# Turning the normalised input: paired 32-bit transposes on TensorE, or 16-bit ones for blocks 0 and 1 and VectorE's word transposes through DRAM for blocks 2 and 3

## The chip, the cores and the metric

The kernel runs on one core of a Trainium2 chip. The metric is the device time of one launch in microseconds (us). The engines are TensorE (PE; its weight loads are shown as PEld), VectorE (DVE), ScalarE (ACT), GpSimd (POOL) and SyncE (SP, which issues the DMAs).

## The reference

One layer with two branches in parallel, on x of 2048 rows by 512 columns in bf16:

```python
xn = layernorm(x)                                   # over the 512 columns
qkv = xn @ wqkv                                     # 512 x 1536; 32 heads of 16
# head-wise, each position attends to 8 positions: itself and 2, 4, ... 14 back
logits = einsum("bhsd,bhswd->bhsw", q, k[pos - 2*w]) * 16**-0.5   # masked where pos - 2*w < 0
o = einsum("bhsw,bhswd->bhsd", softmax(logits), v[pos - 2*w])
h = gelu(xn @ w_gate) * (xn @ w_up)                 # 512 x 1376, tanh form
out = x + o @ wo + h @ w_down                       # 512 x 512 and 1376 x 512
```

## The kernel before

The 2048 rows are four blocks (b) of 512, each two pairs (p = 0 to 7) of 256 rows, each two tiles (t = 0 to 15) of 128 rows. For a block the steps are:

- **Input and layer norm.** `ld_x` loads rows into a slot of XIN (four slots of 256 rows; blocks 2 and 3 also use XIN later for the residual input, `ldxr`). For blocks 0 and 1, VectorE takes the statistics (`bnst`, `bnag`), subtracts the mean (`sub`) and scales (`norm`). For blocks 2 and 3, ACT does all of that (lines 746 to 837), and POOL takes the root as a power (`sq`, line 811), whose reciprocal (`rstd`) VectorE forms.
- **Transpose.** `tpx` turns the normalised rows on TensorE (lines 863 to 885) and `evx` copies them to xnT (ACT, line 898). Two neighbouring bf16 columns are read as one 32-bit word, so that two transposes of 128 words turn a tile of 512 columns; the evacuation separates the halves. Feature 4q + k so comes to partition q, and the weights Wqkv, Wg, Wu and Wt are loaded to match: rows 4q to 4q + 3 to partition q. In pair 0 the work is halved (`tpx`, `tpy`; `evx` on ACT, `evy` on VectorE).
- **Projections.** TensorE forms Q, K and V (`mma`, `mmb`, `mmt`, `mmv`, `mm`; lines 941 to 1027), ACT copies them out (`evq`, `evk`, `evv`).
- **Attention.** VectorE multiplies Q with shifted K (`pr`, line 1055, 4.42 us each) and adds (`pa`, `pb`); TensorE adds over heads (`er`); ACT copies the logits out (`lc`). Softmax goes through `d1`, `d2` (VectorE), `exp`, `ln`, `d5` (ACT), `d4`, `d6` (VectorE). The weights go to DRAM (`ss`, pt_scratch) and come back spread over the partitions (`sl`, PT). VectorE multiplies with shifted V (`pv`, line 1207) and adds (`pw`, `pz`; the last of them, line 1227, writes OT).
- **FFN.** `fg` and `fu` on TensorE (line 1245), `gelu` and `uev` on ACT, `h` on VectorE.
- **Output.** TensorE adds `h @ w_down` (`acc...`, line 1337) and `OT @ wo`; in block 3 the latter are tasks of their own at the end (`accw`). ACT copies the sum out (`fe`), VectorE adds x (`fin`), SP stores (`sto`).

Each step is a task on one engine. The program text holds the order of the tasks on each of the five engines, written out (ORDER, line 377). A function (`schedule`, line 169) goes through these orders once, while the program is built, and gives slots of XIN, of the eight PSUM banks and of the other buffers to the tasks in the order in which a model of the durations lets them start; semaphore waits follow from the data and the slots (`assign_sync`). At run time each engine does its list in order.

Of the kernel before, what the change touches and what calls it, by code (L numbers as in the profile page):

```python
# [97 lines left out]
class Graph:  # L98
# [263 lines left out]
    def report(self):  # L362
# [17 lines left out]
        "warm13 warm14 mma0_0 tpx0_1 tpy0_1 mmb0_0 mma0_1 mmt1_0 tpx1_0 mmt1_1 mmt1_2 mmb0_1 tpx1_1 mmt0_2 "  # L380
        "mmt0_3 mmt1_3 mmv0_1 tpx3_0 fg0_0 tpx2_0 fg0_1 fg0_2 fu0_0 fg0_3 mm1_1_0_0 fu0_1 mm1_0_0_0 fu0_2 "
        "fg0_4 mm1_0_2_0 mm1_1_3_0 mm1_0_3_0 mm1_1_2_0 fg0_10 fu0_3 fg1_0 fg0_5 er0_3 mm1_2_3_0 mm1_0_1_0 "
        "mm1_1_1_0 fu0_4 mm1_2_0_0 fu0_5 mm1_2_2_0 fg1_1 fg1_2 fu1_0 fu1_1 fg1_3 mmv0_0 fg1_4 fg1_5 fu1_2 "
        "fu1_3 fg0_6 fg1_6 mmv1_0 fg1_7 fu1_4 fu0_6 mmv1_1 fg0_7 fu0_7 mm1_2_1_0 fg0_8 er1_3 fu0_8 fu1_5 "
        "fg1_8 tpx4_0 fg0_9 fg1_9 fu0_9 fu1_6 tpx5_0 fu1_7 fu1_8 mm2_1_2_0 mm2_0_2_0 mm2_0_0_0 mm2_1_0_0 "
        "mm2_1_3_0 mm2_2_1_0 mm2_0_3_0 mm2_0_1_0 mm2_1_1_0 fu1_9 fg1_10 fg2_0 fg2_1 accd1 fg2_2 accd3 fg2_3 "
        "fu2_0 acca0 fu2_1 fu2_2 accb0 accd2 er2_3 fu2_3 fg2_10 fg2_4 tpx6_0 mm2_2_0_0 tpx7_0 fg2_5 mm2_2_2_0 "
        "fg3_0 mm2_2_3_0 mm3_0_2_0 mm3_0_3_0 mm3_1_2_0 mm3_1_1_0 mm3_0_0_0 fg2_6 mm3_0_1_0 fu2_4 mm3_1_3_0 "
        "fu2_5 fu2_6 fg3_1 mm3_1_0_0 fu3_0 fu3_1 fg3_2 accd7 fg2_7 fu2_7 mm3_2_3_0 acca4 accd6 fg3_3 fg2_8 "
        "mm3_2_0_0 accb4 er3_3 fu3_2 fu3_3 fg3_4 fg3_5 fg2_9 accd5 fu2_8 fu3_4 fg3_6 fu3_5 mm3_2_2_0 fu3_6 "  # L390
        "fg3_7 fu3_7 fu2_9 mm3_2_1_0 fg3_8 fg3_9 fg3_10 fu3_8 fu3_9 acca8 accb8 accd15_0 accd15_2 acca12 "
        "accd11 accd10 accb12 accd9 accd13 accd15_1 accw15_2 accw13 accw15_0 accd14_0 accw12 accw14_0 "
        "accd14_1 accw15_1 accw14_1",
    "act":
        "c_tbl sx1 sq0 negm1 sxx1 evx0_0 sq1 evx0_1 sq2 evq0_0 evx1_0 sq3 evk0_1 evk0_0 evk0_2 evx1_1 evq0_1 "
        "bnst8 sq6 evq0_2 sq4 evq0_3 evk0_3 bnst9 evx3_0 halo1 evx2_0 ve8 gelu0_1 vp8 gelu0_0 bnag8 evk1_0_0 "
        "bnag9 uev0_0 bnst10 uev0_1 sub8 uev0_2 gelu0_4 bnst11 va8 evq1_2_0 gelu0_3 evq1_0_0 ve10 evk1_3_0 "
        "vp10 evk1_2_0 vb8 gelu0_2 uev0_3 uev0_10a gelu0_5 evq1_3_0 gelu0_10 lc0 uev0_10c bnag10 uev0_10b "
        "evk1_1_0 evv1_3_0 exp0 evv0_0_1 uev0_4 bnag11 evq1_1_0 evv1_0_0 ln0 va10 d5_0 uev1_0 uev0_5 uev1_1 "
        "evv1_2_0 gelu1_2 evv0_0_0 gelu1_3 gelu1_0 uev1_2 vb10 gelu1_5 sub9 halo2 sub11 uev1_3 gelu1_4 bnst12 "  # L400
        "gelu1_1 norm9 uev0_6 gelu0_6 evv0_1_1 evv0_1_0 uev1_4 uev0_7 gelu1_6 evv1_1_0 gelu0_7 norm8 gelu1_7 "
        "lc1 sub10 uev1_5 bnst13 evx4_0 norm10 norm11 gelu0_9 uev0_9 uev0_8 evx5_0 gelu0_8 uev1_7 gelu1_8 "
        "uev1_6 ve12 gelu1_9 evk2_2_0 exp1 evk2_3_0 uev1_8 uev1_10b vp12 evk2_0_0 bnag12 evk2_1_0 evq2_0_0 "
        "evq2_1_0 bnag13 evq2_2_0 ln1 bnst14 evq2_3_0 va12 uev1_10a halo3 bnst15 uev1_10c d5_1 ve14 vb12 "
        "sub13 halv1 sub12 vp14 fe1 gelu1_10 gelu2_2 bnag14 sub14 bnag15 gelu2_1 gelu2_0 va14 sub15 vb14 "
        "uev2_0 fe3 fe0 uev1_9 halv2 uev2_2 gelu2_3 uev2_1 norm12 norm13 lc2 uev2_3 norm14 evv2_1_0 norm15 "
        "evx6_0 evx7_0 uev2_10c gelu2_4 evv2_2_0 gelu3_0 uev2_10a fe2 evv2_3_0 gelu2_10 evq3_2_0 gelu2_5 "
        "uev2_10b exp2 evk3_1_0 evv2_0_0 evq3_1_0 evk3_2_0 uev2_4 evk3_3_0 ln2 d5_2 evq3_3_0 evq3_0_0 uev3_1 "
        "uev2_5 uev2_6 evk3_0_0 fe7 uev3_0 gelu3_1 uev2_7 gelu2_7 gelu3_2 gelu2_6 fe6 gelu3_3 fe4 evv3_3_0 "
        "lc3 uev3_3 uev3_10c gelu3_5 uev3_2 gelu3_4 uev3_10b exp3 halv3 uev2_8 ln3 d5_3 evv3_0_0 uev3_4 "  # L410
        "uev3_5 gelu2_9 evv3_2_0 fe5 uev3_7 uev3_6 gelu3_6 gelu3_7 gelu2_8 evv3_1_0 uev2_9 gelu3_9 gelu3_8 "
        "uev3_8 uev3_10a uev3_9 gelu3_10 fe8 fe11 fe10 fe9 fe13 fe12",
    "dve":
        "c_wdz bnst0 bnag0 sub0 rstd0 norm0 mean1 sub1 evy0_0 rstd1 norm1 bnst2 bnag2 sub2 rstd2 evy0_1 norm2 "
        "bnst3 bnag3 sub3 rstd3 norm3 bnst6 bnst4 bnst7 bnag4 bnag6 bnag7 bnst5 sub7 bnag5 rstd6 sub6 norm7 "
        "norm6 sub5 rstd4 sub4 norm5 norm4 pr0_0 pr0_1 pa0 pb0 h0_1 mask d1a_0 d1b_0 d1c_0 d2_0 pr1_1 d4a_0 "
        "h0_10 d4b_0 rstd8 d4c_0 h0_0 d6_0 pr1_0 h0_2 pa1 h1_1 h1_0 pb1 rstd10 pv0_0 d1a_1 h0_3 d1b_1 h1_2 "
        "d1c_1 pv0_1 d2_1 pw0_1 h0_4 pw0_2 d4a_1 pz0 d4b_1 h1_3 d4c_1 pr2_0 d6_1 pr2_1 h1_10 pa2 rstd12 pb2 "
        "pv1_0 rstd14 h2_0 d1a_2 fin0 d1b_2 h1_4 h2_1 d1c_2 pv1_1 d2_2 pw1_1 d4a_2 pw1_2 d4b_2 fin3 d4c_2 pz1 "
        "h2_10 d6_2 pr3_1 pr3_0 fin2 pa3 h2_2 pb3 pv2_1 d1a_3 d1b_3 h2_3 d1c_3 d2_3 pv2_0 d4a_3 h3_0 d4b_3 "  # L420
        "d4c_3 fin4 h3_1 d6_3 pw2_1 h3_2 pw2_2 pz2 fin7 h3_3 h2_4 fin5 h3_4 h3_10 pv3_0 pv3_1 fin8 pw3_1 fin6 "
        "pw3_2 fin11 pz3 fin9 fin1 fin10 fin13 fin15_0 fin15_2 fin12 fin14_0 fin15_1 fin14_1",
    "pool":
        "c_ones c_onef c_id c_vnpad c_eps c_mhalf c_e8a c_e8b c_e8c c_e8d c_ktpad c_mask0 c_mask1 c_utz sq8 "
        "sq10 sq12 sq14",
    "sp":
        "ld_x0_0 ld_x0_1 ld_wq ld_x1_0 ld_wk ld_x3 ld_x1_1 ld_x2 ld_wv ld_x4 ld_wg0 ld_wu0 ld_wu1 ld_x5 "
        "ld_wg1 ld_wt0 ld_wt1 ld_wt2 ldxr0 ld_wd0 ss0_0 ss0_1 ss0_3 ld_x6 ld_x7 ss0_2 sl0_0 ld_wd1 ldxr3 "
        "sl0_1 sl0_2 sl0_3 ld_wo ss1_1 ss1_0 ss1_3 ss1_2 sl1_1 sl1_0 sl1_3 sl1_2 ldxr2 ss2_1 ldxr9 ss2_0 "
        "ss2_3 ldxr4 ss2_2 sto0 sto3 sl2_2 sl2_0 sto2 sl2_3 ldxr7 ldxr10 sl2_1 ldxr5 ldxr12 sto4 ldxr11 ss3_0 "  # L430
        "ss3_3 ss3_2 ss3_1 ldxr13 sl3_0 sl3_1 sl3_3 ldxr14 ldxr6 ldxr8 ldxr1 sl3_2 sto5 sto8 sto7 sto6 sto11 "
        "ldxr15 sto9 sto10 sto1 sto13 sto15_0 sto15_2 sto12 sto14_0 sto15_1 sto14_1",
# [19 lines left out]
def bass_parallel_sum__sliding_local_dilated__glu_gated_geglu__prompt_kernel(nc, A_x, A_wqkv, A_wo, B_x, B_w_gate, B_w_up, B_w_down, out, dbg=None, cfg=None):  # L452
# [31 lines left out]
    TPF = cfg.get("TPF", 1.5)  # L484
# [12 lines left out]
    with contextlib.ExitStack() as es:  # L497
        block = es.enter_context(nc.Block())

        def sb(name, shape, dt):  # L500
            return es.enter_context(nc.sbuf_tensor(name, shape, dt))
# [8 lines left out]
        KT = sb("KT", [128, 2, 4, 528], BF)  # L510
        cf = sb("cf", [128, 128], F32)
# [40 lines left out]
        XINF = XIN.bitcast(F32)  # L552
        PD = nc.dram_tensor("pt_scratch", (4 * 32, 8 * 512), BF, kind="Internal")
# [30 lines left out]
        I_wo = Item("Wo")  # L584
        I_cf = Item("cf")
# [30 lines left out]
            channel_multiplier=1), rd=[I_cf], wr=[I_cf], prio=PC)  # L616
        G.task("pool", "c_mhalf", 0.1, lambda e: e.memset(mhalf[:, :], 0.5), wr=[I_mhalf], prio=PC2)
# [38 lines left out]
        for i, nm in enumerate(("q", "k", "v")):  # L656
            def mk(i=i):
                return lambda e: e.dma_start(
                    Wqkv[:, :, i * 512:(i + 1) * 512],
                    A_wqkv[:, i * 512:(i + 1) * 512].rearrange("(p k) n -> p k n", k=4))  # L660
            t_w = G.task("sp", "ld_w" + nm, 0, mk(), wr=[(I_wq, (nm, 0)), (I_wq, (nm, 1))] if i == 0 else [(I_wq, nm)],
                         prio=(-958, -957.5, -898)[i], nbytes=(900 if i == 0 else 512) * 1024)
            t_ld["w" + nm] = t_w
        I_wt = Item("Wt")
        for (nm, Wx, I_w, src, h) in (("g", Wg, I_wg, B_w_gate, 0), ("u", Wu, I_wu, B_w_up, 0),
                                      ("g", Wg, I_wg, B_w_gate, 1), ("u", Wu, I_wu, B_w_up, 1)):
            def mk(Wx=Wx, src=src, c=slice(640 * h, 640 * h + 640)):
                return lambda e: e.dma_start(Wx[:, :, c], src[:, c].rearrange("(p k) n -> p k n", k=4))
# [4 lines left out]
        for (i, src, c0, c1, o) in ((0, B_w_gate, 1280, 1376, 32), (1, B_w_up, 1280, 1312, 0),  # L673
                                    (2, B_w_up, 1312, 1376, 128)):
            def mk(src=src, c0=c0, c1=c1, o=o):
                return lambda e: e.dma_start(Wt[:, :, o:o + c1 - c0],
                                             src[:, c0:c1].rearrange("(p k) n -> p k n", k=4))
# [22 lines left out]
        for p in range(NP):  # L700
            b = p // 2
            base = LN_BASE[b] + (p % 2) * 10
            it_x = Item("xin%d" % p, P_xin, "x")
            XINI.append(it_x)
# [116 lines left out]
            for t2 in range(2):  # L821
                t = 2 * p + t2
                if p >= PACT:
# [7 lines left out]
                    def mk_nm(t=t, t2=t2, it=it_x):  # L831
# [3 lines left out]
                    G.task("act", "norm%d" % t, 0.6, mk_nm(), rd=[(it_x, t2), (I_rstd, t)], wr=[(it_x, t2)],  # L835
# [15 lines left out]
                def mk_nm(t=t, t2=t2, it=it_x):  # L851
# [3 lines left out]
                t_of["norm%d" % t] = G.task("dve", "norm%d" % t, 0.27, mk_nm(), rd=([I_xs] if t == 1 else xp(it_x, p, t2)) + [(I_rstd, t)],  # L855
# [596 lines left out]
```

## Time and profile before

| | |
|---|---|
| Median of 3 runs | 186.99 us (186.55 to 187.34) |
| The profiled execution | 186.91 us, of which the span of the profile is 185.2 |
| TensorE | 178.7 us busy, 1050 matmuls; clock 1.0 throughout |
| VectorE | 170.3 us busy, 156 instructions |
| ACT | 137.7 us busy, 276 instructions |
| DMA | 20748 packets, 18.03 MB |

Times inside the profile count from the start of the span. A busy TensorE is not yet a TensorE at its peak, because matmuls overlap: what it costs is seen from the start of one group to the start of the next. The same holds, by some 0.08 us an instruction, for VectorE and ACT. Behind an instruction in a timeline stands the idle time of its engine just before it and what ended that, in square brackets.

### The profile page before, as it was taken

What the parts mean: (1) busy time and instruction counts of PE and PEld (TensorE: products, weight loads), DVE (VectorE), ACT (ScalarE), POOL (GpSimd) and SP (SyncE); (2) the same over time, 40 slices, a digit from 0 to 9 for tenths busy, and PEclk for the clock granted to TensorE, in tenths of its full rate; (3) what the DMA queues carried; (4) which work ended last, traced back from release to release, by engine and by line L of the source; (5) the groups of instructions that cost most, each with busy time, mean ns of one, the idle gap of its engine ahead of it and who ended that gap; (6) DMA issues with size and microseconds to landing.
All of it is one profiled execution on the core that took longest, in us unless ns stands there. A gap on an engine that the chain in (4) does not pass through costs nothing.

```text
span 185.2 us, 2759 instructions
## 1 busy us (share of the span) xinstructions
PE 178.7 (97%) x1050; PEld 94.1 (51%) x1068; DVE 170.3 (92%) x156; ACT 137.7 (74%) x276; POOL 20.3 (11%) x22
## 2 busy tenths in 40 slices
PE   8699999999999999999999999999999999999994
PEld 2598444445464555444444554444444444644473
DVE  3789999499998999999989999999999999999943
ACT  5579999899999999999977998537468799112110
POOL 5000003100270000009920000000000000000000
PEclk9999999999999999999999999999999999999999
DMA  3999500360538000002610100146300167501152
GB/s 105 335 349 365 139 2 0 90 226 14 159 100 281 10 0 4 0 2 57 172 58 0 28 0 0 49 124 187 125 0 4 43 147 211 168 0 60 41 168 74
DMA packets 20748, 18.03 MB, mean 97 GB/s; under 512 B 7328, under 2 KB 18560, under 8 KB 20736
## 3 DMA queue, kind: packets, MB, share of 16 engines
q1 hardware_dynamic: 20736, 17.86, 31.6%
q8 instruction: 8, 0.13, 0.3%
q14 instruction: 4, 0.03, 0.1%
HBM read 14.71 MB, written 3.15 MB: 96 GB/s over the span
## 4 chain that ended last, share of the span: by engine, by line
PE 75%; ACT 9%; POOL 6%; DMA 3%; issue 3%; DVE 2%; SPq 1%; DVEq 0%
PE PS L1245 31%; PE PS L1337 21%; PE PS L1024 14%; POOL sq L811 6%; DMA Wqkv<-in_A_wqkv_dram 3%; PE PS L941 3%; PE PS L999 2%; PE PS L869 2%; ACT QT L1035 1%; DVE UNI L1074 1%; PE PS L1284 1%; ACT UT L1300 1%; ACT XS L794 1%; SPq L709 1%; ACT XIN L832 1%
## 5 line engine op out<-in xcount | busy, mean ns | idle before, releaser
L1337 PE MATMUL PS<-Wd,HT 128*128 128x512 bf16 (+2 forms) x204 | 40.1, 345 | 0.2
L1245 PE MATMUL PS<-xnT,Wg 128*128 128x512 bf16 x152 | 38.4, 379 | 0.7 <-ACT VN L1009 0.2
L1245 PE MATMUL PS<-xnT,Wu 128*128 128x512 bf16 x159 | 38.8, 379 | 0.1
L1207 DVE TENSOR_TENSOR UNI<-VN,PT 128x8192 f16<-128x8192 bf16 x8 | 35.3, 4417 | 0.7 <-DMA PT<-pt_scratch 0.7
L1055 DVE TENSOR_TENSOR UNI<-QT,KT 128x8192 f16<-128x8192 bf16 x8 | 35.2, 4415 | 0.0
L1024 PE MATMUL PS<-xnT,Wqkv 128*128 128x512 bf16 x141 | 33.7, 379 | 0.3 <-ACT QT L1035 0.2
L1337 PEld LDWEIGHTS PS<-Wd,HT 128*128 128x128 bf16 x209 | 19.6, 98 | 18.7
L1255 ACT ACTIVATE GG<-PS 128x512 bf16<-128x512 f32 x40 | 23.7, 615 | 4.7 <-DVE HT L1269 3.2
L1370 ACT ACTIVATE OB<-PS 128x512 bf16<-128x512 f32 x14 | 8.4, 598 | 25.3 <-DMA out_dram<-OB 17.2
L1262 ACT ACTIVATE UU<-PS 128x512 bf16<-128x512 f32 x40 | 23.4, 604 | 3.9 <-PE PS L1245 3.8
L811 POOL TENSOR_TENSOR sq<-ve,mhalf 128x2 bf16<-128x2 f32 x4 | 17.8, 4447 | 72.6 <-ACT ve L807 72.6
L1245 PEld LDWEIGHTS PS<-xnT,Wu 128*128 128x128 bf16 x160 | 15.4, 98 | 19.1 <-issue 1.3
L1245 PEld LDWEIGHTS PS<-xnT,Wg 128*128 128x128 bf16 x160 | 15.6, 98 | 17.7 <-ACT VN L1009 0.7
L1024 PEld LDWEIGHTS PS<-xnT,Wqkv 128*128 128x128 bf16 x144 | 16.3, 114 | 15.0 <-ACT GG L1255 0.4
L1067 DVE TENSOR_TENSOR UNI<-UNI 128x8192 f16<-128x8192 f16 x4 | 17.7, 4418 | 0.0
L1216 DVE TENSOR_TENSOR UNI<-UNI 128x8192 f16<-128x8192 f16 x4 | 17.7, 4416 | 0.0
L1337 PE MATMUL PS<-Wo,OT 128*128 128x512 bf16 (+2 forms) x75 | 16.1, 345 | 0.1
L1269 DVE TENSOR_TENSOR HT<-GG,UU 128x1024 bf16<-128x1024 bf16 x20 | 13.4, 682 | 0.0
L898 ACT ACTIVATE xnT<-PS 128x1024 bf16<-128x1024 bf16 (+2 forms) x10 | 8.0, 810 | 3.9 <-PE PS L869 2.3
L1337 PEld LDWEIGHTS PS<-Wo,OT 128*128 128x128 bf16 x76 | 7.0, 98 | 6.8 <-issue 0.4
L1074 DVE TENSOR_TENSOR UNI<-UNI 128x4096 f16<-128x4096 f16 x4 | 9.1, 2282 | 0.0
L1222 DVE TENSOR_TENSOR UNI<-UNI 128x4096 f16<-128x4096 f16 x4 | 9.1, 2280 | 0.0
(97 smaller groups left out, 192.2 us busy)
## 6 DMA issues: line engine op xcount, KB each, us to landing
PT<-pt_scratch SPq DMA_DIRECT2D x16, 256.0 KB, 4.0
out_dram<-OB SPq DMA_DIRECT2D x14, 128.0 KB, 1.8
XIN<-in_A_x_dram SPq DMA_DIRECT2D x12, 128.0 KB, 2.8
Wqkv<-in_A_wqkv_dram SPq DMA_DIRECT2D x3, 512.0 KB, 5.9
XIN<-in_A_x_dram SPq DMA_DIRECT2D x6, 256.0 KB, 5.7
Wg<-in_B_w_gate_dram SPq DMA_DIRECT2D x2, 640.0 KB, 7.5
Wu<-in_B_w_up_dram SPq DMA_DIRECT2D x2, 640.0 KB, 8.8
Wd<-in_B_w_down_dram SPq DMA_DIRECT2D x1, 1280.0 KB, 7.3
```

What stands on the lines that cost most here:

```text
L811: "pool", "sq%d" % t, 5.0, lambda e, t=t, n=n: e.tensor_tensor(out=sq[:, t:t + n], in0=ve[:, t:t + n], in1=mhalf[:, 0:n], op=ALU.pow),
L1024: ins = e.matmul(PS[:, 512 * it.slot:512 * it.slot + 512], lhsT=wcols(which, kt, g), rhs=xnT[:, itx.slot, kt, :], start=(kt == 0), stop=(k ...
L1055: return lambda e: e.tensor_tensor(out=UNI[:, it.slot:it.slot + 2, :, :], in0=bass.AP(QT, (itq.slot * 4 + 2 * h) * 512, [[NQT * 4 * 512, 1 ...
L1067: return lambda e: e.tensor_tensor(out=UNI[:, i0.slot:i0.slot + 2, :, :], in0=UNI[:, i0.slot:i0.slot + 2, :, :], in1=UNI[:, i1.slot:i1.slo ...
L1074: return lambda e: e.tensor_tensor(out=UNI[:, i0.slot, :, :], in0=UNI[:, i0.slot, :, :], in1=UNI[:, i0.slot + 1, :, :], op=ALU.add)
L1207: return lambda e: e.tensor_tensor(out=bass.AP(UNI, ito.slot * 4096, [[NUNI * 4096, 128], [2048, 4], [512, 4], [1, 512]]), in0=bass.AP(VN, ...
L1216: return lambda e: e.tensor_tensor(out=UNI[:, i0.slot:i0.slot + 2, :, :], in0=UNI[:, i0.slot:i0.slot + 2, :, :], in1=UNI[:, i1.slot:i1.slo ...
L1245: ins = e.matmul(PS[0:M, 512 * it.slot:512 * it.slot + 512], lhsT=Wx[:, kt, j * 128:j * 128 + M], rhs=xnT[:, itx.slot, kt, :], start=(kt = ...
L1255: return lambda e: e.activation(out=GG[:, ito.slot, q, :], in_=PS[:, 512 * it.slot:512 * it.slot + 512], func=ACTF.Gelu_apprx_tanh)
L1262: return lambda e: e.activation(out=UU[:, ito.slot, q, :], in_=PS[:, 512 * it.slot:512 * it.slot + 512], func=ACTF.Identity)
L1269: return lambda e: e.tensor_tensor(out=HT[:, ito.slot, j - 1:j + 1, :], in0=GG[:, ig.slot, :, :], in1=UU[:, iu.slot, :, :], op=ALU.mult)
L1337: ins = e.matmul(PS[:, 512 * it.slot:512 * it.slot + CW], lhsT=(OT[:, ito.slot, q, ti * 128:(ti + 1) * 128] if kind == "o" else HT[:, ith. ...
```

## The change

- **Blocks 0 and 1** are transposed in 16 bits: four transposes of 128 columns a tile instead of two of 128 words, with an identity in bf16 (`c_idb`, a cast on POOL). The evacuations read plain columns. `norm0` and `norm1` are split into halves of 256 columns.
- **Blocks 2 and 3** no longer pass TensorE. ACT's `norm` writes its row in a permuted order into a second slot of XIN (`xw`), VectorE transposes 32 x 32 words (`tr4` to `tr7`, one for each pair), SP stores the result to a scratch tensor in DRAM in four parts (`xs`, runs of 64 bf16) and loads it again (`xl`), and ACT's `evx` separates the halves of the words on the way to xnT, from SBUF instead of PSUM.
- **The weights** Wqkv, Wg, Wu and Wt are loaded with rows q, 128 + q, 256 + q and 384 + q on partition q.
- **The orders** of all five engines are written anew. Of them the prediction uses these parts:

```diff
 "pe" after:  ... mm1_1_3_0 fg0_5 fu0_5 er0_3 ... fu3_8 fg3_9 fu3_9 acca8 accb8 acca12 accd10 accd15_2 accb12
              accd15_0 accd14_0 accd11 accd9 accd13 accw15_2 accw15_0 accw13 accw14_0 accw12 accd14_1
              accw14_1 accd15_1 accw15_1
 "act" after: ... uev1_6 evx5_0 evv1_0_0 gelu1_7 ... sub15 norm15 halo3 fe1 fe3 uev1_10c uev1_10b uev1_10a
              fe0 gelu1_10 gelu1_8 gelu2_1 gelu2_2 uev2_0 uev2_1 evv2_0_0 evv2_1_0 gelu1_9 uev2_2 lc2
              uev2_10c evx6_0 fe2 evx7_0 ...
 "dve" after: ... norm0a norm0b ... bnst3 bnag3 evy0_1 sub3 ... pr0_0 pr0_1 pa0 pb0 h0_0 rstd8 mask h0_1 d1a_0
              d1b_0 tr4 d1c_0 d2_0 pr1_0 d4a_0 d4b_0 d4c_0 h0_2 rstd10 d6_0 pr1_1 pa1 tr5 pb1 h0_3 h1_0 h1_1
              pv0_0 ... h1_2 d4c_1 h1_3 tr6 d6_1 rstd14 pr2_0 tr7 pa2 h1_10 pb2 pv1_1 ... fin3 ... fin0 ...
              fin6 ... fin2 ... fin5 ... fin4 pz2 ... fin7 pv3_0 fin1 fin8 pw3_1 fin11 pw3_2 fin10 pz3 fin9 ...
 "sp" after:  ... ld_wg0 ld_wu0 ld_x5 ld_wg1 ld_wu1 ld_wt0 ld_wt1 ld_wt2 xs4_2 xs4_0 ld_x6 xs4_3 xs4_1 ld_wd0
              ss0_1 ... xl4 sl0_0 sl0_2 sl0_1 xs5_0 xs5_1 xs5_2 xs5_3 sl0_3 ld_x7 ldxr0 xl5 xs6_0 ss1_0 ss1_1
              ss1_2 xs6_1 xs6_2 ss1_3 xs6_3 xs7_1 sl1_3 sl1_2 xl6 xs7_2 xs7_3 xs7_0 sl1_0 sl1_1 xl7 ...
```

The core of the code:

```diff
+        ident = sb("ident", [128, 128], BF)
+        XD = nc.dram_tensor("xt_scratch", (8 * 256, 512), BF, kind="Internal")
+        G.task("pool", "c_idb", 0.65, lambda e: e.tensor_copy(out=ident[:, :], in_=cf[:, :]),
 ...
-                    A_wqkv[:, i * 512:(i + 1) * 512].rearrange("(p k) n -> p k n", k=4))
+                    A_wqkv[:, i * 512:(i + 1) * 512].rearrange("(k p) n -> p k n", p=128))
 ...  (the same for Wg, Wu and Wt)
+            it_xw = Item("xw%d" % p, P_xin, "x") if b in TR_DVE else None      # TR_DVE = (2, 3)
 ...  (norm of blocks 2 and 3, on ACT)
+                            return lambda e: e.activation(
+                                out=XIN[:, itw.slot, t2, :].rearrange("q (c i e) -> q e i c", i=32, e=2),
+                                in_=XIN[:, it.slot, t2, :].rearrange("q (e i c) -> q e i c", e=2, i=32),
+                                func=ACTF.Identity, scale=rstd[:, t:t + 1])
 ...
+            if it_xw is not None:
+                G.task("dve", "tr%d" % p, d_dve(512, 1.04), lambda e, it=it_x, itw=it_xw: e.transpose(
+                    out=XINF[:, it.slot, :, :].rearrange("q t (c i) -> q (t c i)", c=8),
+                    in_=XINF[:, itw.slot, :, :].rearrange("q t (c i) -> q c t i", c=8)),
+                for a in range(4):
+                    G.task("sp", "xs%d_%d" % (p, a), 0.64, lambda e, it=it_x, a=a, p=p: e.dma_start(
+                        bass.AP(XD, p * 131072 + 64 * a, [[4096, 32], [256, 16], [1, 64]]),
+                        XIN[32 * a:32 * a + 32, it.slot, :, :].rearrange("q t (c f) -> q (t c) f", f=64)),
+                t_xl = G.task("sp", "xl%d" % p, 0.5, lambda e, itw=it_xw, p=p: e.dma_start(
+                    XIN[:, itw.slot, :, :], bass.AP(XD, p * 131072, [[512, 128], [65536, 2], [1, 512]])),
+                G.task("act", "evx%d_0" % p, 1.05, lambda e, itw=it_xw, itx=XTI[b], o=o: e.activation(
+                    out=xnT[:, itx.slot, :, o:o + 256].rearrange("q (e s) c -> q s c e", e=2),
+                    in_=XIN[:, itw.slot, :, :].rearrange("q s (c e) -> q s c e", e=2), func=ACTF.Identity),
+                continue
 ...  (blocks 0 and 1)
-                            for s in range(2):
-                                c0 = 512 * it.slot + s * 128 * n + q * 128
-                                ins = e.transpose(PS[:, c0:c0 + 128], XINF[:, ito.slot, t2, s:s + 255:2],
-                                                  cf[:, :])
+                            for kt in range(4):
+                                c0 = 1024 * (it, it2)[kt // 2].slot + kt * 128 * n + q * 128
+                                ins = e.transpose(PSB[:, c0:c0 + 128], XIN[:, ito.slot, t2, kt * 128:(kt + 1) * 128],
+                                                  ident[:, :])
```

## The prediction

> **What bounds the kernel now.** First the page, for what is full and where:
>
> ```profile
> PE 178.7 (97%) x1050; PEld 94.1 (51%) x1068; DVE 170.3 (92%) x156; ACT 137.7 (74%) x276; POOL 20.3 (11%) x22
> ...
> DVE  3789999499998999999989999999999999999943
> ACT  5579999899999999999977998537468799112110
> PEclk9999999999999999999999999999999999999999
> ```
>
> Matmuls overlap (379 ns is one's duration, but four 512-column ones start every 0.86 us), so 97% alone proves little. DVE is full from slice 4 to slice 38, and ACT to slice 20. Three engines run close together, so the next view is the gaps: the idle time in VectorE's timeline between its first big product (line 1055, start 16.79) and the last sum of the attention (line 1227, end 176.03).
>
> ```profile
> 34.01 0.29 DVE L1121 TENSOR_TENSOR PS<-PS,mask 32x128 f32<-32x128 f32 x1 [1.09 <-PE PS L1098]
> 35.47 0.43 DVE L1132 TENSOR_TENSOR SU<-PB 128x512 bf16<-128x512 bf16 x1 [1.17 <-ACT PB L1127]
> 43.78 0.69 DVE L1176 TENSOR_TENSOR PB<-EX,rc 128x1024 bf16<-128x1024 f16 x1 [0.44 <-ACT rc L1172]
> 57.95 4.42 DVE L1207 TENSOR_TENSOR UNI<-VN,PT 128x8192 f16<-128x8192 bf16 x1 [0.73 <-DMA PT<-pt_scratch]
> 93.33 0.17 DVE L782 RECIPROCAL rstd<-sq 128x2 f32<-128x2 bf16 x1 [0.58 <-POOL sq L811]
> ...
> 174.81 1.21 DVE L1227 TENSOR_TENSOR OT<-UNI 128x2048 bf16<-128x2048 f16 x1
> ```
>
> In 159 us VectorE waits 4.0 us (1.09 + 1.17 + 0.44 + 0.73 + 0.58); the last 118 us hold one wait. Then TensorE's timeline around that end:
>
> ```profile
> 171.18 5.53 PE L1337 MATMUL PS<-Wd,HT 128*128 128x512 bf16 x32
> 176.54 1.69 PE L1337 MATMUL PS<-Wo,OT 128*128 128x128 bf16 x12
> ```
>
> The product with Wo of block 3 needs that sum and starts at 176.54, with no gap on TensorE before it. VectorE was done 0.5 us earlier; a hand-over takes about 0.2, so 0.3 us is spare. TensorE sets the end, VectorE is 0.3 us behind it as a second bound: time taken off TensorE brings nothing unless VectorE follows.
>
> **The change part by part.** *Blocks 2 and 3 leave TensorE.* The chain of waits holds
>
> ```profile
> 62.25 0.47 PE PS L869 x4
> ```
>
> Four 32-bit transposes turn 256 rows in 0.47 us. Four such pairs go: TensorE -1.88 us. *Blocks 0 and 1 in 16 bits*: eight transposes for four. Sixteen 128-column 16-bit matmuls (line 941) take about 0.90 us in steady state, 0.056 each, so eight cost 0.45 for 0.47: nothing. The Trainium skill ("TensorE: Matmul & The Clock Gate", Part 4: PE-mode transpose) speaks against doubling their number: it gives some 275 ns for a 16-bit transpose inside a kernel. The trace agrees on a single one (283 ns median at line 869), but four end in 0.47 us because they overlap. At 275 ns unoverlapped, the sixteen of block 1 would add some 3.5 us; I leave that out.
>
> *VectorE gets four word transposes* (tr4 to tr7) of 512 32-bit words. The trace has none. Low end: a two-input 16-bit operation on 512 columns, 0.42 us. High end: twice the one-word-per-step price, 1.2. Taken: 0.69, like line 729 (512 columns, 684 ns); line 1381's rows give the same (284 ns at 128, 419 at 256: 1.05 ns per column over 150). Neighbours overlap by 0.08, so 0.61 each, +2.44 us. All four stand ahead of the last attention sum. In VectorE's new order eleven final adds (fin) stand ahead of it where nine did: 2 x 0.34 = +0.68. The split norms of rows 0 to 255 cost 0.17 more each (348 ns whole, 150 for one column at line 742, so about 250 a half), but run before the 1.41 us wait for the input's fourth tile: free; uncovered, 0.34. The copy evy0_1 (0.40, 0.33 of it unoverlapped) moves behind that wait: +0.33 before the first big product. Sum: +3.45.
>
> *What the new order absorbs.* tr4 stands behind the waits for mask and logits, tr5 and tr7 behind a 4.3 us operation, tr6 behind two products of the FFN: none fills an old gap. But h0_1 now stands in the 1.17 wait (0.6), and with a transpose more ahead of pv0_0 the 0.73 wait shrinks by 0.6. Absorbed: 1.2; at most all 4.0, at least 0. Last sum: 176.03 + 3.45 - 1.2 = 178.3.
>
> *The tail on TensorE.* Of the work after that sum (6.05 us now, 176.54 to 182.59), accd14_0 (eleven 256-column matmuls, 1.2 us) moves ahead and accd15_1 (eleven of 128, 0.62) behind: 5.5 us left. TensorE would be ready for it at 176.54 - 1.88 + 1.2 - 0.62 = 175.2, three us before VectorE: so VectorE decides. End of TensorE: 178.3 + 0.2 + 5.5 = 184.0, against 182.6: +1.4 us. What follows (last add, store) is the same.
>
> *The trip through DRAM.* Each pair adds four stores of 64 KB and a 256 KB load. Nearest rows: the pt_scratch stores (64 KB in runs of 256 bytes, 2.2 us to landing, 0.6 to issue), PT loads 4.0, x loads 5.7. One trip: 0.7 + 4 x 0.6 + 2.2 + 0.5 + 4.0 = 9.8 us at 4.0, 11.5 at 5.7, where now the evacuation follows the transposes at once. It is off the path if the statistics run ten us earlier; ACT's new order puts some twenty instructions of about 0.5 between norm15 and evx7_0, so I take 0. On SP's queue the twenty issues (12 us) are in line with others: the stores of pair 7 stand ahead of block 1's PT loads (sl1_3, sl1_2) and wait for tr7. Behind tr7, VectorE has pa2, h1_10 and pb2 (4.34 + 0.33 + 2.2 = 6.9 us) before pv1_1 needs them, and 1.8 of issues plus 4.0 of landing make 5.8: covered by 1.1 us. Stores of pair 4 stand before Wd's load, used 40 us later. Runs of 128 bytes may land slower than 256; +2 us would break that cover. On ACT, a late load stops evx4_0 to evx7_0; behind evx5_0 stand evv1_0 and gelu1_7, whose PSUM banks TensorE then waits for. *ACT*: line 898's copies (1.02 us) read SBUF instead of PSUM; line 1150 (1024 columns from SBUF, 1.06) says +0.04. The norms write in steps of 128 bytes, which no row shows: 0 to a doubling of the 0.42 us that 512 columns take (line 898: 1.02 at 1024, 0.60 at 512): 8 x 0.42 = 3.4 us on an engine full to slice 20; taken 0, like line 832's 0.73. The skill ("SBUF — State Buffer", Door 1) says each access that crosses to another 16-byte line pays a penalty; no run here shows it, and by it ACT would go towards the 3.4.
>
> *Weights in tiles of 128 rows*: runs keep their length and only their order in DRAM changes. Wd is already loaded like that (1280 KB in 7.3 us), Wqkv in rows of four (4.6 to 6.9 for 512 KB under load): taken 0. TensorE waits 1.3 us on Wqkv at the start, so bounds are -0.6 and +1.0. The 16-bit identity costs POOL one cast (0.21 us for 32 columns at line 626, 0.1 of it fixed, so some 0.55 for 128), done by about 2.1; the first transposes start at 4.93: hidden by 2.8 us, and a longer cast would delay them by what it has over that.
>
> **The rivals.** *A, TensorE sets the end and is relieved (faster).* Decides from the point where the new order absorbs nearly all 4.0 us of VectorE's waits. With 2.6 absorbed the end does not move; with 3.5 it is 0.9 us earlier, with all 4.0 it is 1.4: 185.5 us. TensorE's own floor lies below that (175.2 + 5.5 = 180.7, -1.9). For: the orders are written anew on every engine. Against: two of the five waits (rc, POOL's power) stand where no new work goes. *B, it cancels*: 1.7 to 3.5 absorbed, 186.0 to 187.8, about 187. *C, the trip or the strided norms show*: if landings are 2 us late, pv1_1 waits about 1 and the first matmuls of block 3 about 1 more, on top of the forecast: 190.3. For: today block 3 has no lead (norm15 ends at 101.95, its transposes start at 102.00). Against: the margins above.
>
> **How the numbers follow.** The sum stands against the profiled execution, 186.91 us (span 185.2, 1.71 around it), 0.08 under the median 186.99. Forecast: 186.91 + 1.4 = 188.3. Its own range, 0.6 to 1.7 absorbed: 187.8 to 188.9 on the waits alone; transposes at the far 1.2 would add 4 x 0.5 = 2.0 and reach 190.3. About 0.5% (0.93 us) is what a measurement of this kernel can tell from no change. Chances: forecast 0.51, A 0.18, B 0.18, C 0.13. So faster 0.18, same 0.18, slower 0.64. Leaving out half of A and the far half of C, the range is 185.7 to 190.3.
>
> **What would show it.** Right: PE's busy sum about 2 us lower in a longer span; four transposes on DVE near 0.7 us; line of pz3 ending near 178; TensorE now idle in front of the last Wo products or at waits for VectorE. The DMA packets grow by at least 8192 runs of 128 bytes. Wrong: pz3 ending before 177 with DVE's waits gone (A or B); a wait of DVE on PT, or of ACT and PE on xt_scratch's loads, over 1 us, or norms over 1 us (C); TensorE's first Wqkv matmuls more than 0.5 us later, which would be the weights.

## The result, and the profile after

The changed kernel takes 217.65 us (median of 4, 214.88 to 221.44) where the one before, run beside it, takes 186.92. Two of the four executions lie more than 1.5% above the fastest and count as slow, so all comparisons here use the other two, 215.7 us on average: ratio 1.154, interval 1.145 to 1.163, 28.8 us slower. The forecast was 188.3 in a range up to 190.3. The direction was right and the size was wrong by 27 us. The profiled execution of the changed kernel took 218.77 us (span 217.1), 3 us more than that average.

The head of its page, for comparison with the head of the page before:

```profile
PE 187.5 (86%) x1068; PEld 91.8 (42%) x1068; DVE 174.0 (80%) x162; ACT 166.9 (77%) x276; POOL 15.8 (7%) x23
...
PE   8899987899494769999279934999999999999995
...
DVE  4799992899584848963789796179999989999973
ACT  6599999999999989699996898879635776740121
PEclk9999999999999958999859995799999999999999
```

VectorE worked 3.7 us more than before (174.0 against 170.3), ACT 29.2 us more (166.9 against 137.7), in the same number of instructions (276). TensorE and VectorE, full before, now have holes, between slices 7 and 26; in the same slices ACT is at 8 or 9 nearly throughout. The costliest groups show where ACT's time is (busy us, then mean ns of one):

```profile
L841 ACT ACTIVATE XIN<-XIN,rstd 128x512 bf16<-128x512 bf16 x8 | 20.5, 2624 | 0.1
L901 ACT ACTIVATE xnT<-XIN 128x1024 bf16<-128x1024 bf16 x4 | 19.1, 4775 | 0.0
```

The same work in the kernel before (min/median/max in ns):

```profile
L832 ACT ACTIVATE XIN<-XIN,rstd x8: 708/732/778, 53.5 to 101.2; 128x512 bf16<-128x512 bf16 x8
L898 ACT ACTIVATE xnT<-PS x10: 384/1018/1025, 5.4 to 102.8; 128x1024 bf16<-128x1024 bf16 x6, 128x256 bf16<-128x256 bf16 x2, 128x512 bf16<-128x512 bf16 x2
```

Line 841 is the norm of blocks 2 and 3, which writes its row in the permuted order: 2624 ns, where line 832 before took a median of 732. Line 901 is evx, which separates the halves of the words: 4775 ns, where a copy of 1024 columns at line 898 took 1018. So eight norms cost 8 x (2.62 - 0.73) = 15.1 us more and four evx 4 x (4.78 - 1.02) = 15.0: 30.1 us, the whole of ACT's increase (29.2) and about the size of the loss (28.8).

That this work is on the path is seen in the chain that ended last, by engine and line, with ACT at 39% of the span where it had 9%:

```profile
PE 51%; ACT 39%; DVE 4%; issue 3%; DMA 1%; SPq 0%; ACTq 0%; DVEq 0%
```

and in some of its steps in order of time (start, us, engine, line):

```profile
72.54 4.65 ACT xnT L901
...
96.55 4.78 ACT XIN L841 x2
...
128.43 4.65 ACT xnT L901
```

VectorE's largest waits (total us, times, longest) name ACT as releaser: the norm itself, and what stands behind the two lines in ACT's list:

```profile
DVE HT L1321 <- ACT UU L1314: 8.1, 2, 4.9
DVE XIN L888 <- ACT XIN L841: 7.8, 3, 3.7
```

TensorE's longest wait, 6.40 us for evx, is the start of block 3's projections, in its timeline:

```profile
133.12 6.85 PE L1076 MATMUL PS<-xnT,Wqkv 128*128 128x512 bf16 x20 [6.40 <-ACT xnT L901]
```

Neither engine waits for the scratch tensor's loads or for PT anywhere.

### The profile page after: what moved, and what is told of

Same layout as the page of the kernel before. It is cut to its first block, busy times and chain, and to the rows that moved or that the text cites. A ratio compares the mean times of both kernels' runs of the same rounds, so it can differ in the third digit from the quotient of the medians.

```text
span 217.1 us, 2812 instructions
## 1 busy us (share of the span) xinstructions
PE 187.5 (86%) x1068; PEld 91.8 (42%) x1068; DVE 174.0 (80%) x162; ACT 166.9 (77%) x276; POOL 15.8 (7%) x23
## 4 chain that ended last, share of the span: by engine, by line
PE 51%; ACT 39%; DVE 4%; issue 3%; DMA 1%; SPq 0%; ACTq 0%; DVEq 0%
PE PS L1389 21%; PE PS L1297 16%; PE PS L1076 12%; ACT XIN L841 9%; ACT xnT L901 7%; ACT GG L1307 4%; ACT UU L1314 3%; DVE UNI L1107 2%; ACT XIN L833 2%; ACT XS L802 2%; ACT XS L756 1%; ACT PB L1179 1%; ACT xnT L951 1%; ACT L1307 1%; DMA XIN<-in_A_x_dram 1%
## 5 line engine op out<-in xcount | busy, mean ns | idle before, releaser
L1076 PE MATMUL PS<-xnT,Wqkv 128*128 128x512 bf16 x144 | 39.1, 423 | 12.0 <-ACT xnT L901 6.4
L1297 PE MATMUL PS<-xnT,Wg 128*128 128x512 bf16 x160 | 39.1, 379 | 6.1 <-ACT UU L1314 3.4
L1389 PE MATMUL PS<-Wd,HT 128*128 128x512 bf16 (+2 forms) x209 | 41.7, 353 | 0.0
L1314 ACT ACTIVATE UU<-PS 128x512 bf16<-128x512 f32 x40 | 24.4, 630 | 5.4 <-PE PS L1297 3.2
L1297 PEld LDWEIGHTS PS<-xnT,Wu 128*128 128x128 bf16 x160 | 15.1, 98 | 20.2 <-ACT GG L1307 0.9
L841 ACT ACTIVATE XIN<-XIN,rstd 128x512 bf16<-128x512 bf16 x8 | 20.5, 2624 | 0.1
L1389 PE MATMUL PS<-Wo,OT 128*128 128x512 bf16 (+2 forms) x76 | 17.1, 359 | 2.6 <-ACT OB L1422 2.6
L901 ACT ACTIVATE xnT<-XIN 128x1024 bf16<-128x1024 bf16 x4 | 19.1, 4775 | 0.0
L819 POOL TENSOR_TENSOR sq<-ve,mhalf 128x2 bf16<-128x2 f32 x4 | 13.0, 3242 | 77.4 <-ACT ve L815 56.1
L1087 ACT ACTIVATE KT<-PS 128x512 bf16<-128x512 f32 x12 | 7.1, 590 | 5.1 <-PE PS L1076 5.1
```

The lines of the kernel that those rows point to most:

```text
L841: return lambda e: e.activation(out=XIN[:, itw.slot, t2, :].rearrange("q (c i e) -> q e i c", i=32, e=2), in_=XIN[:, it.slot, t2, :].rearr ...
L901: G.task("act", "evx%d_0" % p, 1.05, lambda e, itw=it_xw, itx=XTI[b], o=o: e.activation(out=xnT[:, itx.slot, :, o:o + 256].rearrange("q (e ...
L1076: ins = e.matmul(PS[:, 512 * it.slot:512 * it.slot + 512], lhsT=wcols(which, kt, g), rhs=xnT[:, itx.slot, kt, :], start=(kt == 0), stop=(k ...
L1297: ins = e.matmul(PS[0:M, 512 * it.slot:512 * it.slot + 512], lhsT=Wx[:, kt, j * 128:j * 128 + M], rhs=xnT[:, itx.slot, kt, :], start=(kt = ...
L1314: return lambda e: e.activation(out=UU[:, ito.slot, q, :], in_=PS[:, 512 * it.slot:512 * it.slot + 512], func=ACTF.Identity)
L1389: ins = e.matmul(PS[:, 512 * it.slot:512 * it.slot + CW], lhsT=(OT[:, ito.slot, q, ti * 128:(ti + 1) * 128] if kind == "o" else HT[:, ith. ...
```

## The experiments

The theory after this result: ACT pays for the order in which it writes, and nearly all of the loss is that. The rivals: the price comes from contention with VectorE's transposes or the DMAs; or the rest of the change (new orders, more VectorE work, the trip) carries a good part of the loss.

### The price of an order, alone on the chip (e1)

One kernel without the layer: it runs ACT and VectorE instructions of these shapes, each pattern twice, with nothing beside them.

```diff
+ e.activation(out=B[:, 0:64*511+1:64], in_=A[:, 0:512], func=ACTF.Identity, scale=rs[:, 0:1])   # L51; other lines: other steps
+ e.activation(out=B.."q (c i e) -> q e i c", in_=A.."q (e i c) -> q e i c", ...)                # L57, the norm as changed
+ e.activation(out=.."q (e s) c -> q s c e", in_=A.."q (s c e) -> q s c e", ...)                 # L60, evx as changed
```

> Leaves the whole computation out: ScalarE and VectorE each copy 512 columns (128 partitions, 16 bits, SBUF to SBUF) with a write step or a read step of 1 to 64 elements, and then in the two orders of the changed norm and evacuation, alone on the chip and one after the other. Theory (the write order costs ScalarE, nothing else): dense 0.73 us; written 8 columns at 128 bytes apart as in the changed norm 2.6 us; the 1024-column evacuation with its two halves written alternately 4.8 us, and 1.05 us with the same data written in runs and read at 4 bytes' step. Steps in reading cost nothing. Rival (contention: other engines and DMAs slow the writes in the full kernel): alone, the scattered forms take under 1.2 us. What step the price begins at is open: 16 bytes by the rule on lines of 16 bytes, 4 or 8 bytes otherwise.

Groups by line (busy us of the two, then mean ns of one); lines 45 to 51 write with a step of 1, 2, 4, 8, 16, 32 and 64 elements of two bytes:

```profile
L45 ACT ACTIVATE B<-A,rs 128x512 bf16<-128x512 bf16 x2 | 1.4, 722 | 67.2 <-DVE rs L28 67.2
L46 ACT ACTIVATE B<-A,rs 128x512 bf16<-128x512 bf16 x2 | 1.7, 864 | 0.1
L47 ACT ACTIVATE B<-A,rs 128x512 bf16<-128x512 bf16 x2 | 2.9, 1427 | 0.1
L48 ACT ACTIVATE B<-A,rs 128x512 bf16<-128x512 bf16 x2 | 5.1, 2556 | 0.1
L51 ACT ACTIVATE B<-A,rs 128x512 bf16<-128x512 bf16 x2 | 5.1, 2570 | 0.1
...
L54 ACT ACTIVATE B<-A,rs 128x512 bf16<-128x512 bf16 x2 | 2.4, 1194 | 0.1
L57 ACT ACTIVATE B<-A,rs 128x512 bf16<-128x512 bf16 x2 | 5.1, 2567 | 0.1
L60 ACT ACTIVATE B<-A 128x1024 bf16<-128x1024 bf16 x2 | 9.4, 4710 | 0.1
L61 ACT ACTIVATE B<-A 128x1024 bf16<-128x1024 bf16 x2 | 2.1, 1056 | 0.1
```

The price nearly doubles with the step from 4 to 8 and from 8 to 16 bytes (864, 1427, 2556 ns) and then stays flat up to 128 bytes (2570). That fits a price for each move of the writes to another 16-byte line: at 16 bytes and more, each element is on another line than the one before it, and (2556 - 722) over the 448 moves more than the 64 of a dense row is 4.1 ns a move on top; over all 512 it is 5.0 ns each, fixed cost included. At shorter steps a move costs less (3.7 ns at 8 bytes, 2.2 at 4). The number of lines touched is not what counts: the changed norm touches the 64 lines of a dense row and no others, but moves with every element, and alone takes 2567 (2624 in the kernel). The changed evx takes 4710 (4775); with its two inner loops exchanged, so that it writes runs, evx takes 1056 (L61). Its 1024 moves instead of 128 come to the same 4.1 ns each. Nothing runs beside them here, so contention falls as a cause. Reading pays less: 1194 ns at steps of 16 bytes (L54), 746 at 8 bytes. I had expected steps in reading to cost nothing; that holds up to 8 bytes only.

### The write orders alone, in the kernel before (e2)

```diff
 (norm8 to norm15)
-    out=XIN[:, it.slot, t2, :], in_=XIN[:, it.slot, t2, :],
+    out=XIN[:, it.slot, t2, :].rearrange("q (c i e) -> q e i c", i=32, e=2), in_= (the same),
 (evx of blocks 2 and 3)
-    out=xnT[...].rearrange("q (s e) c -> q s e c", e=2), in_=PSB[...].rearrange("q (s c e) -> q s e c", ...)
+    out=xnT[...].rearrange("q (s e) c -> q s c e", e=2), in_=PSB[...].rearrange("q (s c e) -> q s c e", ...)
```

Each element is read and written where it was; only the order in which ACT steps through them is the change's. (The norm, which works in place, here also reads in steps of 128 bytes, where the change reads a dense row; in e1 such reads alone take 1152 ns, well below the writes.)

> The kernel before, with only the order in which ScalarE writes changed, values the same: norm8 to norm15 in place with steps of 128 bytes, and the evacuations of pairs 4 to 7 with the halves written alternately. No DRAM trip, no transpose on VectorE, old orders. Theory: eight norms at 2.6 instead of 0.73 and four evacuations at 4.8 instead of 1.02, +30 us of ScalarE; 205 to 217 us. Rival (the DRAM trip, SP's queue or the new orders cost the 30 us): 187 to 190 us.

Measured: 215.01 us (214.71 to 215.18) against 187.18, ratio 1.150 (1.147 to 1.152). The two lines from its trace (min/median/max in ns):

```profile
L832 ACT ACTIVATE XIN<-XIN,rstd x8: 2621/2722/2931, 53.8 to 119.1; 128x512 bf16<-128x512 bf16 x8
...
L899 ACT ACTIVATE xnT<-PS x10: 384/1024/5091, 5.4 to 125.8; 128x1024 bf16<-128x1024 bf16 x6, 128x256 bf16<-128x256 bf16 x2, 128x512 bf16<-128x512 bf16 x2
```

ACT's sum goes to 166.3 us (before 137.7), and 28.6 us more on ACT make 27.8 more in the time. Without transposes on VectorE, without the trip and without new orders, nearly the whole loss (28.8) is there.

### The changed kernel with evx writing runs (e3)

```diff
-    out=xnT[...].rearrange("q (e s) c -> q s c e", e=2), in_=XIN[...].rearrange("q s (c e) -> q s c e", e=2)
+    out=xnT[...].rearrange("q (e s) c -> q s e c", e=2), in_=XIN[...].rearrange("q s (c e) -> q s e c", e=2)
```

> The changed kernel with the four evacuations evx4 to evx7 writing each half as a run and reading at a step of 4 bytes; values the same. Theory: each 4.8 becomes about 1.05, ScalarE -15 us, time 201 to 204. Rival (the price is the load of the scratch tensor that they wait for): unchanged at 215 to 218.

Measured: 202.61 us (201.41 to 203.79), ratio 1.083 (1.077 to 1.090) to before. One exchange of two loops, with the same values in the same places, gives back 13.1 us of the 15.0 that the four instructions cost. They take a median of 1052 ns now; the norms still take 2597, and VectorE's transposes still wait 10.0 us in all in front of them, as in the changed kernel (7.8 behind the norms and 2.2 behind a short copy that follows the last of them):

```profile
DVE XIN L888 <- ACT XIN L841: 10.0, 4, 3.7
```

### The norm stepping in shorter strides as well (e5)

```diff
 (e3's edit, and in the norm)
-    out=XIN[...].rearrange("q (c i e) -> q e i c", ...), in_=XIN[...].rearrange("q (e i c) -> q e i c", ...)
+    out=XIN[...].rearrange("q (c i e) -> q e c i", ...), in_=XIN[...].rearrange("q (e i c) -> q e c i", ...)
```

The innermost loop now writes in steps of 4 bytes and reads in steps of 16.

> The changed kernel, values the same, with evx4 to evx7 written in runs and norm8 to norm15 in the order that writes at 4 bytes' step and reads at 16 (1.20 us in the run of patterns, against 2.56 as changed and 0.72 dense). Theory (the price is the number of 16-byte lines written): norms 1.2, ScalarE 3.8 us over the kernel before, time 187 to 191. Rival (the permutation itself or the DRAM trip costs the rest): norms stay near 2.6 or the time stays over 195.

Measured: 188.84 us (188.58 to 189.0), ratio 1.011 (1.007 to 1.015).

```profile
L841 ACT ACTIVATE XIN<-XIN,rstd x8: 1206/1253/1274, 32.3 to 88.7; 128x512 bf16<-128x512 bf16 x8
```

The same permutation at 1253 ns instead of 2604: of the 28.8 us, 26.9 are gone, with no part of the change given up.

### The norm in natural order (e6)

```diff
 (e3's edit, and in the norm)
-    out=XIN[...].rearrange("q (c i e) -> q e i c", ...), in_=XIN[...].rearrange("q (e i c) -> q e i c", ...)
+    out=XIN[:, itw.slot, t2, :], in_=XIN[:, it.slot, t2, :]
```

> The changed kernel with norm8 to norm15 not permuted (dense writes) and evx4 to evx7 in runs; blocks 2 and 3 then pair features with the wrong weights, and only the time is read. What is left is what my sum priced: TensorE -1.88, four word transposes on VectorE, the DRAM trips, the weights and the new orders. My sum said 188.3 and had 0 for the weights, which measured -1.2: 187.1, between 185.5 and 189. Rival (the DRAM trip or SP's queue hurts by itself): over 189.

Measured: 185.29 us (184.98 to 185.89), ratio 0.992 (0.990 to 0.995): 1.6 us *faster* than before (186.86 beside it), just below the range that was expected. The head of its page:

```profile
PE 177.6 (97%) x1050; PEld 92.0 (50%) x1068; DVE 172.7 (94%) x162; ACT 138.1 (75%) x276; POOL 14.8 (8%) x23
```

and VectorE's timeline, its two waits left before the last attention sum, and that sum:

```profile
32.88 0.29 DVE L1172 TENSOR_TENSOR PS<-PS,mask 32x128 f32<-32x128 f32 x1 [0.53 <-PE PS L1149]
34.26 0.42 DVE L1183 TENSOR_TENSOR SU<-PB 128x512 bf16<-128x512 bf16 x1 [0.50 <-ACT PB L1178]
...
174.19 1.21 DVE L1278 TENSOR_TENSOR OT<-UNI 128x2048 bf16<-128x2048 f16 x1
```

With ACT's sum back at 138.1 the loss is gone. VectorE does 2.4 us more than before and ends the sum 0.6 earlier, at 175.40: of its 4.0 us of waits 1.0 are left. The weights alone bring 1.2 us (e4, below), so some 0.4 of the 1.6 is left for the transposes on VectorE, the trip and the new orders together, which is within the intervals. The gain is not one that the change's kernel could collect as written, because its pairing of words needs the permutation; what a norm in natural order would need elsewhere (rows of the weights in another order, another layout of the scratch tensor) was not built.

### The weights alone (e4)

```diff
-    A_wqkv[...].rearrange("(p k) n -> p k n", k=4)
+    A_wqkv[...].rearrange("(k p) n -> p k n", p=128)      (the same for Wg, Wu and Wt; all else as before)
```

> The kernel before with only the weights Wqkv, Wg, Wu and Wt loaded with rows q, 128 + q, 256 + q, 384 + q on partition q; the transposes stay as they were, so features and weights are paired wrongly and only the time is read. My prediction's term: 0, between -0.6 and +1.0 us. In the changed kernel TensorE's first matmuls on Wqkv began earlier than before, so the theory says -0.5 to 0: 186.4 to 187.0. Rival (rows 384 KB apart load slower): +1 us or more.

Measured: 186.0 us (185.47 to 186.42), ratio 0.993 (0.991 to 0.996): 1.2 us faster than 187.18, more than expected. The profiled executions are 0.7 apart (186.24 and 186.91). TensorE's timeline has the first product with Wqkv 0.57 us earlier, with no wait; it started at 6.47 after 0.74 of waiting:

```profile
5.90 0.64 PE L955 MATMUL PS<-xnT,Wqkv 128*128 128x128 bf16 x8
```

Behind a second wait on Wqkv 0.24 of that lead is left (8.73 for 8.97), and at the end it is 0.67: the last product with Wo starts at 181.10 instead of 181.77. In between VectorE waits 3.5 us instead of 4.0: its waits of 0.73 on PT and of 0.58 behind POOL are gone, and two of 0.28 and 0.52 behind ACT are new. The loads of Wg and Wu land 0.6 and 0.8 us sooner (6.9 and 8.0 us against 7.5 and 8.8), but so does that of Wd, which the edit leaves alone (6.7 against 7.3); of the three loads of Wqkv the quickest takes 3.9 us for 4.6 and the median 6.0 for 5.9. Which of these makes the 1.2 us was not settled.

### Sixteen-bit transposes for all four blocks, and these weights (e7)

The kernel before, in its own orders, with the change's code for blocks 0 and 1 used for blocks 2 and 3 as well, and its weights; no transposes on VectorE, no trip.

```diff
-    TR_DVE = cfg.get("TR_DVE", (2, 3))
+    TR_DVE = cfg.get("TR_DVE", ())           (in the changed kernel; ORDER of the kernel before, with norm0a, norm0b, norm1a, norm1b, c_idb)
```

> The first and third part of the change alone, in the old orders: all four blocks turned by TensorE in 16 bits (eight transposes a pair for four), weights with rows q, 128 + q, 256 + q, 384 + q; no word transposes, no DRAM trip. Values right. Theory: transposes equal (0.45 for 0.47 us a pair), weights -1.2: 185.8 to 186.4. Rival (16-bit transposes do not overlap, 275 ns each): +10 us or more on TensorE, over 190.

Measured: 185.45 us (184.93 to 186.14), ratio 0.993 (0.990 to 0.995): faster than both kernels, and below the expected 185.8 to 186.4. In TensorE's timeline eight transposes take what four 32-bit ones took (0.64 at line 869 before):

```profile
15.14 0.61 PE L917 MATMUL PS<-ident,XIN 128*128 128x128 bf16 x8
```

The time is that of e4 within the intervals, so the doubled number of transposes costs nothing that can be measured; the gain is the weights'.

### More work on VectorE, nothing else (e8)

```diff
+ for q in range(9): G.task("dve", "trx%d" % q, ..., e.transpose(out=TRO[:, :], in_=WgF[:, 0, 0:192]))   (the kernel before; nine of them, at four places without idle time)
```

> The kernel before with nine word transposes of 192 columns added on VectorE in its full stretches (two or three at a time, before pw0_1, pw1_1, pr3_1, pw2_1), nobody waits for their result: VectorE +2.5 to 3 us, nothing else changed. Step tested: VectorE is a second bound 0.3 us behind TensorE. Theory: +2 to +2.5 us, 189 to 189.7. Rival (VectorE has slack somewhere behind them): under 188.

Measured: 188.58 us (188.09 to 189.99), ratio 1.011 (1.007 to 1.015): +1.7 us for 2.8 us more of VectorE's busy sum (173.1 against 170.3), under the expected 189 to 189.7 and above the rival's 188. In the profiled execution (189.17 us, above the median) VectorE's last attention sum ends at 178.72 instead of 176.03; 0.45 of these 2.7 us is a later start of the first big product (17.24 for 16.79). TensorE's Wo products that need it start at 178.78 instead of 176.54. On the way TensorE waits for VectorE twice, 0.34 us each, which it did not in the kernel before; the first of these lines is the wait for block 2's sum:

```profile
PE PS L1343 <- DVE OT L1233: 0.3, 1, 0.3
PE PS L1097 <- DVE UNI L1080: 0.3, 1, 0.3
```

So VectorE is a second bound close behind TensorE: work put where it has no idle time shows for the most part. Block 2's sum ends at 158.57 and the waiting product starts at 158.62, so a hand-over for which TensorE stands idle takes 0.05 us, not 0.2, and the 0.5 us by which VectorE was ahead in the profile before leave some 0.45 of spare, not 0.3.

## Why the prediction was wrong

ACT's work and the time, in one table (the two durations are medians of their lines, ACT busy is from each profile, the time is the median, for the changed kernel the average named with the result):

| kernel | norm, evx (ns) | ACT busy (us) | time (us) |
|---|---|---|---|
| before | 732, 1018 | 137.7 | 186.9 |
| changed, norm in natural order (e6) | 722, 1058 | 138.1 | 185.3 |
| changed, short steps (e5) | 1253, 1052 | 142.0 | 188.8 |
| changed, evx in runs (e3) | 2597, 1052 | 152.3 | 202.6 |
| before, with the write orders (e2) | 2722, up to 5091 | 166.3 | 215.0 |
| changed | 2604, 4777 | 166.9 | 215.7 |

- **The step that failed: the ACT term.** It was two terms. The norms' writes in steps of 128 bytes were bounded at "0 to a doubling of the 0.42 us", 3.4 us for eight, and taken as 0; they measured +1.9 us each, 15.1. The doubling had no reason behind it. The order of evx's writes was not seen at all: the text priced only the change of source from PSUM to SBUF (+0.04 us) and missed that the new inner loop jumps between two halves of xnT with every element; it measured +3.76 us each, 15.0. So a term of 0 to 3.6 was 30.1.
- **The cover.** Taking 0 also needed ACT to have room. It had none: in the 90 us from 20 to 110 of the profile before,

```profile
20.00:110.00 90.00, 89.08 (x482) 44.76 (x490) 85.82 (x60) 85.56 (x177) 17.75 (x4) 1.00 0.21 64
```

  ACT, the fourth engine in this line, is busy 85.56 us, as full as VectorE (85.82). The prediction said that ACT is full to slice 20, and then looked for the path on TensorE and VectorE alone. ACT's work there came out in the time at near its price: 28.6 us of work made 27.8 of time in e2, 14.6 less made 13.1 less from the changed kernel to e3, and 10.3 less made 13.8 less from e3 to e5. That the last is more than its price shows that not all of it is ACT's own time: TensorE's granted clock goes from 0.958 to 1.0 in the same step (see the last section). A sum of ACT's extra work that meets the loss so closely is in part luck.
- **The rule that was set aside.** The Trainium skill ("SBUF — State Buffer", Door 1) was quoted with its penalty for each access that crosses to another 16-byte line, and set aside, because no run showed it. It was right in kind: in e1 the price grows up to a step of 16 bytes and is flat from there on. The page's rule gave no size, and ours came from an arbitrary cap. Where the page says that two hits to a line are needed for full bandwidth, two are not enough for ACT's writes: at two to a line (step of 8 bytes) they take 1427 ns for 722, at four 864. ACT's reads agree (746 at two to a line).
- **Rival C and the signs.** "Norms over 1 us" stood among the signs of rival C, and is what the trace shows, but C's 190.3 was built of landings, and no case carried the norms' cost into its time. The landings came as priced: stores of the scratch tensor 2.2 us, its loads 3.5 (taken 4.0; in e6 2.6 and 4.2), and nobody waits for them. The packets grew by 9536, where at least 8192 was named.
- **VectorE's sum.** The transposes were right: 711 ns each against 0.69. The absorption was wrong: 1.2 us taken, and in e6, where ACT doesn't interfere, 3.0 of the 4.0 us of waits are gone (mask 1.09 to 0.53, PB 1.17 to 0.50, rc, PT and POOL's to nothing), two of these at places that the text had called out of reach. With the first big product 0.65 us earlier, the last sum comes 0.6 earlier instead of 2.3 later, and TensorE goes on to the products that need it at 175.59 without a gap. So the waits were absorbed as rival A has it, and 185.3 is about A's time (185.5); behind the ACT term it could not show. But A's gain is not shown to be TensorE's relief: e7, with all transposes on TensorE and the old orders, takes 185.45, the same within the intervals. Against e7, taking blocks 2 and 3 off TensorE cancels, as rival B says, and the gain over the kernel before is the weights', 1.2 of the 1.6 us by e4.
- **Weights.** Taken 0 within -0.6 to +1.0; e4 measured -1.2, outside the bound. The bound was drawn from the wait at the start, of which 0.57 us went; what more there is goes with fewer waits of VectorE further on (3.5 us for 4.0). That the earlier start removed those was not shown: in e8, with the weights as before, the wait on PT is gone as well.
- **The hand-over.** The 0.2 us for it was 0.15 too much by e8's row (0.05), which moves the forecast's end by no more than that.
- **16-bit transposes.** "Nothing" was right. The Trainium skill ("TensorE: Matmul & The Clock Gate", Part 4: PE-mode transpose) gives some 275 ns for one; here one lasts 219 ns (line 917, median in e7), and eight that overlap take 0.61 us together. The 283 ns that the prediction set beside it is that of a 32-bit one.

## What to carry to other kernels

Before pricing an instruction whose access pattern changes, count how often its innermost loop moves the writes to another 16-byte line, for ACT and VectorE alike: with every element on another line than the one before, ACT's norm of 512 columns took 2.6 us for 0.72, and its copy of 1024 took 4.7 for 1.06. Where a permutation must be made, put the long step on the reading side and the short one (4 bytes or less) or the run on the writing side; e3 and e5 got 26.9 of 28.8 us back by exchanging loops. And ACT, full in the stretch where the work was added, was on the path there, however idle it was at the end of the kernel: look at the stretch, not at the average.

## What the runs showed that was not expected

- VectorE pays for scattered writes too: a tensor_scalar of 512 columns takes 353 ns dense, 513 at steps of 4 bytes, 1359 at 16 and 1389 at 128 (e1), and reading at steps of 16 bytes takes 672.
- TensorE's granted clock falls when TensorE is starved. Two of its waits in the changed kernel, besides the one of 6.40 us shown with the result:

```profile
68.10 0.62 PE L1143 MATMUL PS<-xnT,Wt 128*32 128x256 bf16 x16 [3.51 <-ACT GG L1307]
77.67 9.86 PE L1076 MATMUL PS<-xnT,Wqkv 128*128 128x512 bf16 x32 [3.23 <-ACT VN L1087]
```

  and windows that hold the matmuls behind all three (the columns are PE, PEld, DVE, ACT and POOL, then the clock):

```profile
66.00:72.00 6.00, 3.90 (x38) 1.89 (x39) 3.01 (x3) 5.97 (x14) 0.00 (x0) 1.00 0.36 109
78.00:84.00 6.00, 6.00 (x17) 2.23 (x16) 5.23 (x3) 5.21 (x16) 3.06 (x1) 0.56 0.00 0
132.00:138.00 6.00, 4.88 (x12) 1.76 (x13) 1.58 (x1) 4.87 (x10) 0.00 (x0) 0.51 0.00 0
```

  After the wait of 6.40 us TensorE has 0.51 of its clock, and 12 matmuls fill 4.88 us; after that of 3.23 it has 0.56, but after that of 3.51 it has 1.00. So the length of the last wait alone does not decide it. The mean clock is 0.953 here and 1.0 before, in e5 and in e6, whose TensorE has no such holes. The Trainium skill ("TensorE: Matmul & The Clock Gate", Part 1) has half clock after at least one idle window of some 3.4 us: the 6.40 agrees with it, the 3.23 is shorter than such a window.

  What this does to the time can be read from the chain that ended last. Behind three waits it holds 32, 15 and 20 matmuls of 512 columns that take 9.86, 5.52 and 6.85 us; twelve elsewhere on that chain take 2.60, 0.217 each. So 22.2 us stand where 14.5 would at that pace, and some 7.7 us of this execution's chain are slow clock. Its span is 33.7 us longer than e6's (217.1 and 183.4), so an estimate of 26 us is left for ACT's 28.8 us of extra work and all else: by this estimate it did not show in full. The time at full clock, with ACT's work as it is, was not measured.
